# Attention followed by a gated feed-forward: q and k transposed by DMA through DRAM, exact causal widths, and a hand-written order of the two halves

## The chip, the cores and the metric

One core of one Trainium2 chip. The metric is the device time of one execution in microseconds (us), median of the runs. Engines are named as the profile names them: PE (TensorE matmul), PEld (its weight load), DVE (VectorE), ACT (ScalarE), POOL (GpSimd), SP (SyncE, which issues all DMAs here; SPq is its queue). "Clock" is the share of full speed that PE was granted; "DMA share" is the mean busy share of the core's 16 DMA engines, and in short stretches it came out above 1.

## The reference

```python
# q, k, v: (8, 8, 576, 64)   s: (8, 8, 576)   all float32
scores = q @ k^T / sqrt(64)
cum    = cumsum(max(s, 0), axis=-1)
scores = where(j > i, -1e9, scores + min(-(cum[i] - cum[j]), 0))
x      = softmax(scores) @ v            # -> (4608, 512): 8 batches x 576 rows, 8 heads x 64
g      = x @ w_gate                     # (512, 1536)
out    = (g * sigmoid(g) * (x @ w_val)) @ w_out      # (4608, 512)
```

There are 64 heads of 576 rows and nine feed-forward tiles of 512 rows. A batch is eight heads, and a tile needs the whole batch (or batches) its rows lie in. Both halves meet in a DRAM buffer `xdr`: attention writes its rows there, and each tile reads them back transposed as `xt`. In the profiles `sc` are scores, `av` is softmax times v, `pg` and `pv` are the products of `xt` with the gate and value weights, `ht` is what they combine to, and `py` its product with w_out, copied out as the four blocks y0 to y3 (`ysb`). `kt` and `qt` are k and q transposed; `ks` and `qs` are their scratch in DRAM.

## The kernel before

The decay is folded into the scores: q and k are padded from 64 to 68 columns, so that one matmul gives q·k plus the bias. For each head q and k are cast, transposed on PE through PSUM and copied out; the scores are computed over a row length padded to 640. The order of instructions on the engines is left to the framework's scheduler: the program says "one batch of heads, then the tiles that are ready", and the scheduler mixes them.

```python
def do_head(b, h, stg):
    for name, HT, dstT, ptt in (("k", HTK, KT, ptk_tiles), ("q", HTQ, QT, ptq_tiles)):
        nc.any.tensor_copy(pt[:, 0:4, 0:D], main[:, hh, :, :])        # cast to bf16
        nc.any.tensor_copy(pt[:, 4, 0:D], tailt[:, hh, :])
        nc.gpsimd.tensor_copy(pt[:, :, D:DEXT], HT[:, :, bh, :])      # the decay columns
        for c in range(NCH):                                          # NCH = 5
            nc.tensor.transpose(tps[:, c * 128 : (c + 1) * 128], pt[:, c, :], ident)
        nc.any.tensor_copy(dstT, tps)
    ...
    for ch in SCORE_CHUNKS:                                           # rows padded to 640
        ...  nc.tensor.matmul(sc[...], KT[...], QT[...]);  nc.scalar.activation(Pt, sc, AF.Exp)
    for tj in range(NCH):
        nc.vector.tensor_mul(Pt[:, o : o + 128], Pt[:, o : o + 128], keepmask)
    ...  # 15 av matmuls, reciprocal, scaling, two DMAs to xdr per head

def do_moe_tile(tt):
    for c in range(4):
        nc.sync.dma_start_transpose(xt, xdr[tt * TT : (tt + 1) * TT, c * 128 : (c + 1) * 128])
    ...  # 12 x (4 pg + 4 pv matmuls), then 4 x 12 py matmuls, four output DMAs
```

The softmax here doesn't subtract the row's maximum and nothing guards it: scores larger than these inputs give would overflow.

Of the kernel before, what the change touches and what calls it, by code (L numbers as in the profile page):

```python
# [19 lines left out]
def kernel(  # L20
# [11 lines left out]
    nc = tc.nc  # L32

    B, H, S, D = q.shape
    BH = B * H
    NT, DM = out.shape
    DF = moe_w_gate.shape[1]

    SP = 640
    NCH = 5  # L40
    AUG = 4
    DEXT = D + AUG
    HGRP = 4

    PT_OFF = []
    o = 0
    for tj in range(NCH):
        PT_OFF.append(o)
        o += SP - 128 * tj
    PT_TOT = o  # L50

    SCORE_CHUNKS = [
        [(0, 0, 512)],
        [(0, 512, 640), (1, 128, 512)],
        [(1, 512, 640), (2, 256, 640)],
        [(3, 384, 640), (4, 512, 640)],
    ]
# [3 lines left out]
    stage = ctx.enter_context(tc.tile_pool(name="stage", bufs=2))  # L61
    head = ctx.enter_context(tc.tile_pool(name="head", bufs=4))
    small = ctx.enter_context(tc.tile_pool(name="small", bufs=4))
    wpool = ctx.enter_context(tc.tile_pool(name="wpool", bufs=1))
    moes = ctx.enter_context(tc.tile_pool(name="moes", bufs=4))
    hpool = ctx.enter_context(tc.tile_pool(name="hpool", bufs=3))
    xtp = ctx.enter_context(tc.tile_pool(name="xtp", bufs=8))

    apsum = ctx.enter_context(tc.tile_pool(name="apsum", bufs=1, space=bass.MemoryType.PSUM))
    mpsum = ctx.enter_context(tc.tile_pool(name="mpsum", bufs=4, space=bass.MemoryType.PSUM))  # L70

    dram = ctx.enter_context(tc.tile_pool(name="dram", bufs=1, space=bass.MemoryType.DRAM))

    ident = const.tile([128, 128], BF16)
    make_identity(nc, ident)
    keepmask = const.tile([128, 128], BF16)
    make_upper_triangular(nc, keepmask, val=1.0, diag=True)

    NPT = 4
    ptk_tiles = [const.tile([128, NCH, 128], BF16, name=f"ptk{i}") for i in range(NPT)]  # L80
    ptq_tiles = [const.tile([128, NCH, 128], BF16, name=f"ptq{i}") for i in range(NPT)]
    for t in ptk_tiles + ptq_tiles:
        nc.vector.memset(t[:, :, DEXT:128], 0.0)

    spos = prep.tile([BH, SP], FP32)
    nc.vector.memset(spos[:, S:SP], 0.0)
    s_sb = prep.tile([BH, S], FP32)
    nc.sync.dma_start(s_sb, s.flatten_outer_dims())
    nc.scalar.activation(spos[:, 0:S], s_sb, AF.Relu)

    cum_a = prep.tile([BH, SP], FP32)
    cum_b = prep.tile([BH, SP], FP32)
    nc.vector.tensor_copy(cum_a, spos)
    srcs = [cum_a, cum_b]
    cur = 0
    shift = 1
    while shift < S:
        src = srcs[cur]
        dst = srcs[1 - cur]
        nc.vector.tensor_add(dst[:, shift:SP], src[:, shift:SP], src[:, 0 : SP - shift])  # L100
        nc.vector.tensor_copy(dst[:, 0:shift], src[:, 0:shift])
        cur = 1 - cur
        shift *= 2
    cum = srcs[cur]

    c8 = srcs[1 - cur]
    nc.scalar.mul(c8, cum, 8.0)
    hi_bf = prep.tile([BH, SP], BF16)
    nc.vector.tensor_copy(hi_bf, c8)
    lo_f = spos  # L110
    nc.vector.tensor_sub(lo_f, c8, hi_bf)
    lo_bf = prep.tile([BH, SP], BF16)
    nc.vector.tensor_copy(lo_bf, lo_f)
    nhi_bf = prep.tile([BH, SP], BF16)
    nc.scalar.mul(nhi_bf, hi_bf, -1.0)
    nlo_bf = prep.tile([BH, SP], BF16)
    nc.scalar.mul(nlo_bf, lo_f, -1.0)

    HTK = prep.tile([128, NCH, BH, AUG], BF16)
    HTQ = prep.tile([128, NCH, BH, AUG], BF16)  # L120
    nc.vector.memset(HTK[:, :, :, 2:4], 1.0)
    nc.vector.memset(HTQ[:, :, :, 0:2], 1.0)

    def transpose_bh_to_s(src_bf, dst, w):
        for c in range(NCH):
            ps = apsum.tile([128, 64], BF16, tag="tp", bufs=1, name="htp")
            nc.tensor.transpose(ps, src_bf[:, c * 128 : (c + 1) * 128], ident[0:64, 0:64])  # L127
            nc.any.tensor_copy(dst[:, c, :, w], ps)

    transpose_bh_to_s(hi_bf, HTK, 0)  # L130
    transpose_bh_to_s(lo_bf, HTK, 1)
    transpose_bh_to_s(nhi_bf, HTQ, 2)
    transpose_bh_to_s(nlo_bf, HTQ, 3)

    def load_group(b, g):
        h0 = g * HGRP
        stg = {}
        for name, src in (("q", q), ("k", k), ("v", v)):
            main = stage.tile(
                [128, HGRP, 4, D], FP32, tag="stg_" + name, name="stg" + name  # L140
            )
            for c in range(4):
                nc.sync.dma_start(  # L143
                    main[:, :, c, :],
                    src[b, h0 : h0 + HGRP, c * 128 : (c + 1) * 128, :].rearrange(
                        "h p d -> p h d"
                    ),
                )
            tail = stage.tile(
                [128, HGRP, D], FP32, tag="stgt_" + name, name="stgt" + name  # L150
            )
            nc.gpsimd.memset(tail[64:128, :, :], 0.0)
            nc.sync.dma_start(
                tail[0:64, :, :],
                src[b, h0 : h0 + HGRP, 512:576, :].rearrange("h p d -> p h d"),
            )
            stg[name] = (main, tail)
        return stg

    GPB = H // HGRP  # L160
    NGRP = B * GPB
    next_stg = load_group(0, 0)

    WG = [wpool.tile([128, DF], BF16, name=f"wg{c}") for c in range(4)]
    WV = [wpool.tile([128, DF], BF16, name=f"wv{c}") for c in range(4)]
    WO = [wpool.tile([128, DM], BF16, name=f"wo{c}") for c in range(12)]

    def load_weight_piece(i):
        if i < 4:
            c = i  # L170
            wtmp = stage.tile([128, DF], FP32, tag="wld", bufs=2, name="wld")
            nc.sync.dma_start(wtmp, moe_w_gate[c * 128 : (c + 1) * 128, :])
            nc.any.tensor_copy(WG[c], wtmp)
            wtmp2 = stage.tile([128, DF], FP32, tag="wld", bufs=2, name="wld2")
            nc.sync.dma_start(wtmp2, moe_w_val[c * 128 : (c + 1) * 128, :])
            nc.any.tensor_copy(WV[c], wtmp2)
        else:
            for c in range(2 * (i - 4), 2 * (i - 4) + 2):
                wtmp = stage.tile([128, DM], FP32, tag="wld3", bufs=2, name="wld3")
                nc.sync.dma_start(wtmp, moe_w_out[c * 128 : (c + 1) * 128, :])  # L180
                nc.any.tensor_scalar_mul(WO[c], wtmp, 0.5)
    NWPIECE = 10

    xdr = dram.tile([NT, DM], BF16, name="xdr")

    def do_head(b, h, stg):
        bh = b * H + h
        hh = h % HGRP
        KT = head.tile([128, SP], BF16, tag="KT", name="KT")
        QT = head.tile([128, SP], BF16, tag="QT", name="QT")  # L190
        for name, HT, dstT, ptt in (
            ("k", HTK, KT, ptk_tiles),
            ("q", HTQ, QT, ptq_tiles),
        ):
            main, tailt = stg[name]
            pt = ptt[(b * H + h) % NPT]
            nc.any.tensor_copy(pt[:, 0:4, 0:D], main[:, hh, :, :])  # L197
            nc.any.tensor_copy(pt[:, 4, 0:D], tailt[:, hh, :])
            nc.gpsimd.tensor_copy(pt[:, :, D:DEXT], HT[:, :, bh, :])
            tps = apsum.tile([128, SP], BF16, tag="tp", bufs=1, name="tps")  # L200
            for c in range(NCH):
                nc.tensor.transpose(  # L202
                    tps[:, c * 128 : (c + 1) * 128], pt[:, c, :], ident
                )
            nc.any.tensor_copy(dstT, tps)  # L205

        vmain, vtail = stg["v"]
        VT = head.tile([128, NCH, D + 1], BF16, tag="VT", name="VT")
        nc.any.tensor_copy(VT[:, 0:4, 0:D], vmain[:, hh, :, :])
        nc.any.tensor_copy(VT[:, 4, 0:D], vtail[:, hh, :])  # L210
        nc.gpsimd.memset(VT[:, :, D], 1.0)

        Pt = head.tile([128, PT_TOT], BF16, tag="Pt", name="Pt")
        for ch in SCORE_CHUNKS:
            width = sum(e[2] - e[1] for e in ch)
            first_tj = ch[0][0]
            sc = apsum.tile([128, 512], FP32, tag="score", bufs=2, name="sc")
            off = 0
            for (tj, ilo, ihi) in ch:
                w = ihi - ilo  # L220
                nc.tensor.matmul(  # L221
                    sc[:, off : off + w],
                    KT[:, 128 * tj : 128 * (tj + 1)],
# [20 lines left out]
        for bi in range(NCH):  # L244
# [27 lines left out]
            ot[0:64, 4, :],  # L272
        )

    TT = 512
    NTT = NT // TT

    def do_moe_tile(tt):
# [105 lines left out]
```

## Time and profile before

| | us |
|---|---|
| time, median of the first 3 runs | 505.06 (504.21 to 507.08) |
| span of the profiled run | 506.3 |
| PE busy | 442.4 (87%) |
| first feed-forward tile begins | 115.7 |
| one tile with eight heads, once PE is full | 49.5 |
| one tile alone | 31.1 |

The prediction below shows the slices and stretches. From the page, these are the engine totals and the groups that the change touches. The columns of a group are: line, engine, operation, output<-input, count, then busy us, mean ns of one, and the idle time just before with what ended it.

```profile
PE 442.4 (87%) x3364; PEld 237.4 (47%) x3364; DVE 319.3 (63%) x991; ACT 298.2 (59%) x665; POOL 53.2 (11%) x248
...
L292 PE MATMUL pg<-xt,wg 128*128 128x512 bf16 x432 | 123.6, 379 | 2.0 <-DMA xt<-xdr 1.5
...
L239 DVE TENSOR_TENSOR Pt<-Pt,keepmask 128x128 bf16<-128x128 bf16 x320 | 64.5, 221 | 16.5 <-ACT Pt L230 14.5
...
L202 PE MATMUL tps<-ident,ptk 128*128 128x128 bf16 x320 | 31.3, 227 | 13.9 <-ACT ptk L197 13.5
...
L205 DVE COPY KT<-tps 128x640 bf16<-128x640 bf16 x49 | 23.8, 487 | 13.5 <-PE tps L202 13.1
```

The row to keep in mind is the first group: over the whole run PE waited only 1.5 us for `xt`. The transposes (L202, here those of k) and their copies out of PSUM (L205) are the work that the change moves to the DMA engines, and the masks (L239) go from DVE to POOL.

### The profile page before, as it was taken

What the parts mean: (1) busy time and instruction counts of PE and PEld (TensorE: products, weight loads), DVE (VectorE), ACT (ScalarE), POOL (GpSimd) and SP (SyncE); (2) the same over time, 40 slices, a digit from 0 to 9 for tenths busy, and PEclk for the clock granted to TensorE, in tenths of its full rate; (3) what the DMA queues carried; (4) which work ended last, traced back from release to release, by engine and by line L of the source; (5) the groups of instructions that cost most, each with busy time, mean ns of one, the idle gap of its engine ahead of it and who ended that gap; (6) DMA issues with size and microseconds to landing.
All of it is one profiled execution on the core that took longest, in us unless ns stands there. A gap on an engine that the chain in (4) does not pass through costs nothing.

```text
span 506.3 us, 10025 instructions
## 1 busy us (share of the span) xinstructions
PE 442.4 (87%) x3364; PEld 237.4 (47%) x3364; DVE 319.3 (63%) x991; ACT 298.2 (59%) x665; POOL 53.2 (11%) x248
## 2 busy tenths in 40 slices
PE   0277743658999999999999999999999999999997
PEld 0144532433445445554555465546554664444443
DVE  8348853645919846983798278828881887174570
ACT  3568865765439527972796289628952984232331
POOL 2013211110001101210121012102100100000000
PEclk9999985969999999999999999999999999999999
DMA  7805779677756751466255715671641121401102
GB/s 167 245 13 123 197 237 170 175 166 182 171 145 144 150 135 49 99 128 161 69 115 126 179 41 116 135 169 41 131 86 65 34 45 34 124 0 37 48 1 83
DMA packets 181124, 57.44 MB, mean 113 GB/s; under 512 B 173840, under 2 KB 173840, under 8 KB 181072
## 3 DMA queue, kind: packets, MB, share of 16 engines
q1 hardware_dynamic: 181072, 56.80, 46.7%
q8 instruction: 26, 0.43, 0.4%
q14 instruction: 26, 0.21, 0.1%
HBM read 37.90 MB, written 14.16 MB: 103 GB/s over the span
## 4 chain that ended last, share of the span: by engine, by line
PE 70%; DMA 10%; ACT 9%; DVE 4%; SPq 4%; issue 2%; ACTq 0%; POOL 0%; DVEq 0%; POOLq 0%
PE py L320 18%; PE pg L292 17%; PE pv L300 16%; PE sc L221 9%; PE tps L202 5%; PE av L247 5%; ACT Pt L230 4%; DMA wld<-in_moe_w_val_dram 3%; DMA wld<-in_moe_w_out_dram 2%; SPq L143 2%; DMA stgq<-in_q_dram 2%; ACT QT L205 1%; DMA stgtq<-in_q_dram 1%; DMA stgk<-in_k_dram 1%; PE htp L127 1%
## 5 line engine op out<-in xcount | busy, mean ns | idle before, releaser
L230 ACT ACTIVATE Pt<-sc 128x512 bf16<-128x512 f32 (+1 forms) x256 | 133.6, 581 | 14.4 <-PE sc L221 12.7
L292 PE MATMUL pg<-xt,wg 128*128 128x512 bf16 x432 | 123.6, 379 | 2.0 <-DMA xt<-xdr 1.5
L300 PE MATMUL pv<-xt,wv 128*128 128x512 bf16 x432 | 120.9, 379 | 0.0
L308 ACT ACTIVATE th<-pg 128x512 bf16<-128x512 f32 x108 | 65.0, 602 | 74.2 <-PE pg L292 69.2
L221 PE MATMUL sc<-QT,KT 128*128 128x128 bf16 (+3 forms) x448 | 87.5, 285 | 11.1 <-ACT QT L205 3.7
L310 DVE SCALAR_TENSOR_TENSOR pp<-th,pg 128x512 bf16<-128x512 bf16 x108 | 73.7, 683 | 35.9 <-ACT th L308 35.5
L320 PE MATMUL py<-wo,ht 128*128 128x512 bf16 x432 | 94.7, 379 | 0.0
L314 DVE TENSOR_TENSOR ht<-pp,pv 128x512 bf16<-128x512 bf16 x108 | 74.1, 686 | 7.8 <-PE pg L292 0.5
L239 DVE TENSOR_TENSOR Pt<-Pt,keepmask 128x128 bf16<-128x128 bf16 x320 | 64.5, 221 | 16.5 <-ACT Pt L230 14.5
L247 PE MATMUL av<-VT,Pt 128*128 128x65 bf16 x960 | 67.9, 198 | 6.9 <-DVE Pt L239 5.5
L328 ACT COPY ysb<-py 128x512 f32<-128x512 f32 x36 | 21.1, 586 | 79.8 <-PE py L320 75.0
L247 PEld LDWEIGHTS <-Pt 128*128 128x128 bf16 x960 | 48.6, 99 | 38.8 <-DVE Pt L239 30.5
L320 PEld LDWEIGHTS <-ht 128*128 128x128 bf16 x432 | 42.2, 98 | 51.0
L221 PEld LDWEIGHTS <-KT 128*128 128x128 bf16 x448 | 42.0, 98 | 50.3 <-issue 34.4
L300 PEld LDWEIGHTS <-wv 128*128 128x128 bf16 x432 | 40.4, 98 | 37.1 <-issue 2.6
L292 PEld LDWEIGHTS <-wg 128*128 128x128 bf16 x432 | 40.7, 98 | 34.9 <-issue 0.9
L197 DVE CAST ptk<-stgk 128x256 bf16<-128x256 f32 x45 | 12.7, 289 | 53.9 <-PE tps L202 48.6
L202 PE MATMUL tps<-ident,ptk 128*128 128x128 bf16 x320 | 31.3, 227 | 13.9 <-ACT ptk L197 13.5
L202 PE MATMUL tps<-ident,ptq 128*128 128x128 bf16 x320 | 35.3, 226 | 2.6 <-ACT KT L205 1.6
L202 PEld LDWEIGHTS <-ptk 128*128 128x128 bf16 x320 | 24.5, 101 | 20.2 <-ACT ptk L197 13.8
L205 DVE COPY KT<-tps 128x640 bf16<-128x640 bf16 x49 | 23.8, 487 | 13.5 <-PE tps L202 13.1
L259 DVE TENSOR_TENSOR ot<-av,recip 128x320 bf16<-128x320 f32 x64 | 31.1, 486 | 0.7 <-DVE Pt L239 0.3
(65 smaller groups left out, 277.2 us busy)
## 6 DMA issues: line engine op xcount, KB each, us to landing
out_dram<-ysb SPq DMA_DIRECT2D x36, 256.0 KB, 2.1
stgq<-in_q_dram SPq DMA_DIRECT2D x64, 128.0 KB, 3.0
stgk<-in_k_dram SPq DMA_DIRECT2D x64, 128.0 KB, 2.9
stgv<-in_v_dram SPq DMA_DIRECT2D x64, 128.0 KB, 2.8
xdr<-ot SPq DMA_DIRECT2D x64, 64.0 KB, 2.3
wld<-in_moe_w_gate_dram SPq DMA_DIRECT2D x4, 768.0 KB, 5.7
wld<-in_moe_w_val_dram SPq DMA_DIRECT2D x4, 768.0 KB, 6.6
wld<-in_moe_w_out_dram SPq DMA_DIRECT2D x12, 256.0 KB, 3.0
```

Of the source, the lines that this page charges most:

```text
L202: nc.tensor.transpose(tps[:, c * 128 : (c + 1) * 128], pt[:, c, :], ident)
L221: nc.tensor.matmul(sc[:, off : off + w], KT[:, 128 * tj : 128 * (tj + 1)], QT[:, ilo:ihi], start=True, stop=True,)
L230: nc.scalar.activation(Pt[:, pt_lo : pt_lo + width], sc[:, 0:width], AF.Exp, scale=0.125,)
L239: nc.vector.tensor_mul(Pt[:, o : o + 128], Pt[:, o : o + 128], keepmask)
L247: nc.tensor.matmul(av[:, bi * (D + 1) : (bi + 1) * (D + 1)], Pt[:, colo : colo + 128], VT[:, tj, :], start=(tj == 0), stop=(tj == bi),)
L259: nc.vector.tensor_mul(ot, av3[:, :, 0:D], recip[:, :, None].to_broadcast([128, NCH, D]),)
L292: nc.tensor.matmul(pg, WG[c][:, ft * 128 : (ft + 1) * 128], xts[c], start=(c == 0), stop=(c == 3),)
L300: nc.tensor.matmul(pv, WV[c][:, ft * 128 : (ft + 1) * 128], xts[c], start=(c == 0), stop=(c == 3),)
L308: nc.scalar.activation(th, pg, AF.Tanh, scale=0.5)
L310: nc.vector.scalar_tensor_tensor(pp, in0=th, scalar=1.0, in1=pg, op0=ALU.add, op1=ALU.mult)
L314: nc.vector.tensor_mul(ht, pp, pv)
L320: nc.tensor.matmul(py, hts[ft][:, ts_ * 128 : (ts_ + 1) * 128], WO[ft], start=(ft == 0), stop=(ft == 11),)
```

## The change

Its intent is to take work off PE, DVE and ACT. (1) q and k of four heads are cast on POOL, written to DRAM scratch and read back by a transposing DMA, in place of PE transposes. (2) Scores are computed over 576 rows and not 640, and the four full diagonal blocks are masked by one POOL select. (3) The scheduler is switched off: the order on every engine, SP's queue included, is that of the program text, with attention running `LAG` = 1.5 heads ahead of feed-forward. The diff also has something that the intent does not name: the rows of a batch go to `xdr` in one pair of DMAs after its last head, and no longer in a pair for each head, and `xt` is one transposing DMA and not four.

```diff
-    SP = 640
+    # exact widths: 1600 columns of scores a head, diagonal blocks together
+    CHUNKS = [
+        [(0, 0, 128), (1, 128, 256), (2, 256, 384), (3, 384, 512)],
+        [(0, 128, 576), (3, 512, 576)],
+        [(1, 256, 576), (2, 384, 576)],
+        [(4, 512, 576)],
     ]
 ...
+    with tc.manual_schedule():
+        def scratch(hb):                        # hb: a group of four heads
+            for C, SC in ((CK, KS), (CQ, QS)):
+                nc.sync.dma_start(SC[hb].rearrange(...), C[hb % 2].rearrange(...))
+        def transposes(hb):
+            nc.sync.dma_start_transpose(KT[hb % 2][:, 0 : HB * S], KS[hb])
+            nc.sync.dma_start_transpose(QT[hb % 2], QS[hb])
 ...
-        for c in range(NCH):
-            nc.vector.tensor_mul(... keepmask)
+            if ci == 0:
+                nc.gpsimd.affine_select(pt[:, 1088:1600], ...)
 ...
+        def side(hb, step):                     # step: which of the four heads
+            if hb + 1 < NHB:
+                if step == 0:
+                    if hb + 2 < NHB:
+                        load_qk(hb + 2)
+                        if hb % 2 == 0:
+                            load_v((hb + 2) // 2)
+                    aug(hb + 1, nc.gpsimd); ...     # casts of k
+                if step == 1:
+                    ...                             # casts of q
+                    scratch(hb + 1)
+                if step == 2:
+                    transposes(hb + 1)
 ...
+        def ffn_items(tt):
+            xt = xtp.tile([128, 4, TT], BF16, tag="xt", name="xt")
+            nc.sync.dma_start_transpose(xt, xdr[tt * TT : (tt + 1) * TT, :])
+            ...                                 # pg, pv, py matmuls, one yield each
+        LAG = 1.5
+        for tt in range(NTT):
+            ...
+            for _ in ffn_items(tt):
+                pump(lo + (hi - lo) * min(1.0, n / span))    # heads in between
```

The five v loads of a batch, the outputs y0 to y3 of a tile, `xdr`, the scratch and `xt` all stand in one queue, SP's, in the order in which this text comes to them. `xt` of a tile is issued when its first item is asked for, and that is after the last output of the tile before.

## The prediction

> **What bounds the kernel now.** I read the page first (busy shares and the forty slices), then a table of three stretches, then the order of time inside a mixed stretch, then the issue queue.
>
> ```profile
> span 506.3 us, 10025 instructions
> PE   0277743658999999999999999999999999999997
> PEclk9999985969999999999999999999999999999999
> ```
>
> The page: TensorE (PE) is full from about slice 10, and ragged before it, with a lowered clock in places. So there are two regimes.
>
> ```profile
> 0.00:126.00 126.00, 68.51 (x656) 42.90 (x657) 72.88 (x270) 81.66 (x185) 21.11 (x97) 0.89 0.68 167
> 126.00:440.40 314.40, 311.71 (x2423) 166.47 (x2422) 213.43 (x674) 196.95 (x448) 32.08 (x151) 1.00 0.47 108
> 440.40:502.60 62.20, 62.20 (x289) 27.99 (x286) 33.02 (x48) 19.02 (x32) 0.00 (x0) 1.00 0.09 35
> ```
>
> Stretches (us, then PE, weight load, DVE, ACT, POOL busy, clock, DMA share, GB/s). Before 126 us PE is half idle and DMA is the busiest (0.68). After it PE sets the end: 311.7 of 314.4 us. The last 62.2 us are two feed-forward tiles alone, 31.1 us each.
>
> ```profile
> 250.05 0.33 PE L202 MATMUL tps<-ident,ptq 128*128 128x128 bf16 x3
> 250.21 0.59 PE L292 MATMUL pg<-xt,wg 128*128 128x512 bf16 x2
> 251.29 0.35 PE L247 MATMUL av<-VT,Pt 128*128 128x65 bf16 x6
> 251.91 0.44 PE L202 MATMUL tps<-ident,ptk 128*128 128x128 bf16 x5
> ```
>
> A busy time is latency and overlaps its neighbours, so I take the spacing. Two 512-column matmuls take 0.59 us and one 0.379, so one costs 0.216 us (0.42 ns a column). Six av take 0.35 us at 0.198 each: 0.030 apart. Five transposes take 0.44 at 0.219: 0.055 apart.
>
> ```profile
> 429.47 5.20 SPq L282 DMA_TRANSPOSE xt<-xdr  x4
> ...
> 429.92 4.26 PE L320 MATMUL py<-wo,ht 128*128 128x512 bf16 x19
> ```
>
> The input of the next tile (xt) is fetched while the py matmuls of this tile still run: it is prefetched. That matters below.
>
> DMA rates, each GB/s over DMA share:
>
> ```profile
> 4.00:20.00 16.00, 1.41 (x7) 0.73 (x8) 12.22 (x37) 7.09 (x21) 1.26 (x6) 1.00 0.88 200
> 65.00:71.00 6.00, 3.95 (x52) 2.42 (x49) 3.75 (x13) 4.46 (x9) 0.86 (x2) 1.00 0.77 237
> 405.00:406.00 1.00, 1.00 (x13) 0.65 (x10) 0.98 (x5) 1.00 (x4) 0.00 (x0) 1.00 0.58 131
> 436.00:439.00 3.00, 3.00 (x16) 1.35 (x15) 0.00 (x0) 0.59 (x1) 0.00 (x0) 1.00 0.41 155
> ```
>
> 256 B loads 227 GB/s, weight loads 308, transposes 226, output writes 378.
>
> [...] The trace agrees for the engines (226 against 227 GB/s with 256 B rows), not for the issue: 1.2 us for 512 rows against 0.5 us for a plain DMA. [...]
>
> ```profile
> 72.00:82.00 10.00, 1.03 (x15) 0.87 (x15) 2.98 (x13) 4.12 (x7) 0.31 (x1) 0.53 1.00 212
> 82.00:89.70 7.70, 5.40 (x43) 3.91 (x44) 3.67 (x19) 5.10 (x12) 1.80 (x10) 0.50 0.71 139
> ```
>
> PE stood 8.3 us there, and the clock stayed at half to 89.7.
>
> **The change part by part.** (1) PE per head. Before: scores 1920 columns x 0.42 ns = 0.81 us, ten transposes 0.55, fifteen av 0.45: 1.81 us. After: 1600 columns 0.68, no transposes, av 0.45: 1.13. A tile (144 matmuls, 31.1 us) with eight heads falls from 45.6 (the trace shows 49.5 per period) to 40.1 us. Over seven such periods that is 66 us of possible gain.
>
> (2) DVE and ACT lose the casts, the KT/QT copies (about 0.5 and 0.7 us, 128 of them) and, to POOL, the masking (320 x 0.22 us). They have slack in the mixed part anyway (DVE 213 and ACT 197 of 314 us), so this only helps. POOL gets one 128x512 and one 128x64 select per head and the casts. A 128x128 select took 0.29 us; my estimate from that is 0.7 us for the large one, 20 to 25 us in a period. It is not the bound.
>
> (3) DMA gains 18.9 MB of scratch writes and 18.9 MB of transposed reads on 56.8 MB. For four heads: k and q loads 1.18 MB at 300 GB/s (taking the weight rate for long rows), 3.9 us; scratch write 3.1; transposes 5.2. For a batch, v 5.2; xdr 1.6; xt 2.3; output 2.8. A batch: 2 x 12.2 + 11.9 = 36 us against 40 us of PE. It fits, if it is spread.
>
> (4) The start. First scores need s, k, q, casts, scratch, and also wait for v0, k1 and q1, which SP issues ahead of the first transposes. The first DMA is issued at 0.7 us and a plain one takes about 1.4 us to begin (2.1 us landing of an output less 0.7 of data); s and k, q (0.5 + 3.9) have landed by 7.5, casts 1.7, so the scratch is issued at 9.2. Then 9.2 + 1.4 + 3.1 + 5.2 + 3.9 + 5.2 + 0.6 = 28.6 us, like now. Then, in SP's order up to the first xt: k2 q2 3.9, v1 5.2, scratch 3.1, four weight pairs 4 x 5.1, transposes 5.2, k3 q3 3.9, scratch 3.1, transposes 5.2, k4 q4 3.9, v2 5.2, xdr 1.6, scratch 3.1, xt 2.3: 66 us. With 5 us for waits between scratch and transposes, feed-forward begins at about 99 us, with 9.5 heads behind it; now it runs densely from 126.
>
> (5) The tile boundary. The order of the built program has, on SP, around each boundary: y0, k, q, v (five DMAs), y1, y2, xdr, two scratch writes, y3, xt. So xt is issued only when y3, the last output of the tile before, has been computed, and PE's next instruction after that tile's last py is pg, which needs xt. PE is in order: attention cannot fill the hole. Floor of the hole: copy of y 0.6, issue 0.4, xt with four times the data of the present one (2.7 us landing, 0.9 of it data, now 2.3) 4.1, and 0.3 for semaphores: 5.5 us. With the load burst: y0 is done 30.5 us into a period, so (copy 0.6, issue 0.4, 1.4 to begin) the queue starts at 33 with y0 0.7, k q 3.9, v 5.2, y1 y2 1.4, xdr 1.6: 46; scratch 3.1 and y3 0.7: 50; xt 2.3 and landing: near 52 against 40.1 of PE, a hole of 12. Some of the y and scratch may be out earlier; I take 10.5 us. [...] Five boundaries have the burst; the sixth has scratch alone (7); the last two have neither (5.5).
>
> Sum: start 99; late wo casts in DVE's order 3; five periods 5 x 52.1 = 260.5; 40.1 + 7 + 1.5 = 48.6; the seventh with 7.5 us of attention 38.6 + 7 = 45.6; 31.1 + 7 = 38.1; last tile and its output 34. Total 528.8; I say 528.
>
> **Rivals.** (a) PE bound throughout, holes negligible: 99 + 7 x 40.1 + 62.2 + 3 = 445 us. For it speaks the saturated PE of now; against it that now xt is prefetched, and here it cannot be. (b) Only the floor of each hole, loads drained early: 99 + 342 + 8 x 5.5 + 3 = 488[...]. For it: DMA totals fit in the period. Against: SP reaches the loads only behind y0. (c) Transposes of 2304 rows take SP longer to issue than my 3.4 us (of the present 1.15 us for 512 rows I take 0.5, a plain issue, as fixed and 0.65 as growing with rows; fully proportional it would be 5.2): k and q then come after the heads that need them, DMA and SP become the bound, about 555 us. (d) POOL three times slower than estimated would hold the av matmuls: above 560.
>
> **Range and chances.** The floors (PE 342, eight holes 44, output 3, a start of at least 80) give 470, so a large gain is nearly excluded. The middle case is 528; (b) is the good end, (c) the bad one. Range 495 to 556. Faster by 2% (under 495): 0.14; within 2%: 0.22; slower: 0.64.
>
> **What would show it.** After: PE busy near 342 us plus about 20 at the start by spacing, and the chain of waits naming xt at eight places. In order of time, between the last py of a tile and the next pg: idle of 5 to 12 us, ended by the xt DMA, longest where v was loaded. SP: y3 just before xt. Clock slices under 9 after 100 us. If pg never waits for xt, step 5 is wrong and 445 to 480 is near; if sc waits for kt or qt inside tiles, (c) holds; if av waits for POOL's pt, (d).

Statements about the chip that no trace or run of this case shows are cut from this text, and the cuts are marked. With them go terms of the forecast. The sum came to 528.8 with 1.5 us for the lowered clock at each of the eight boundaries (within each of the five 52.1, as the 1.5 of the sixth, within the 7 of the last two): 12 us, not worked out from the trace; in the stretch quoted the clock stayed at half for 7.7 us after PE restarted at 82.0. Without them the sum is 516.8, still just over 2% slower. What was measured after stands under "The cold clock" below.

"The trace agrees for the engines" compares two numbers of the trace, 226 GB/s for transposes and 227 for plain loads of 256-byte rows. That a DMA waits behind all that SP issued before it was not isolated by any run; where (4) and (5) add up transfers in SP's order, that is the author's estimate. Other things that the prediction counts on are shown by later runs. PE is in order: at a boundary of the kernel after, the nine `av` matmuls that come behind the first `pg` had their last input, POOL's select, at 193.37 us, and PE stood from 193.4 to 206.19 and ran them only behind that `pg`, at 207.85. The "0.3 for semaphores": the chain of such a floor in the run with more lead alone has 0.32 us between its pieces (0.21, 0.02, 0.05 and 0.04).

## The result and the profile after

| | before | after |
|---|---|---|
| time, median of 4 runs each, us | 505.79 | 548.55 (546.96 to 549.58) |
| ratio, fast runs | 1 | 1.0835 (95%: 1.0798 to 1.0872) |
| span of the profiled run, us | 506.3 | 545.3 |
| PE busy, us | 442.4 | 384.4 |
| mean granted clock of PE in the profiled run | 0.973 | 0.861 |
| DMA bytes, MB | 57.44 | 95.00 |

A ratio here is made from the fast runs of both kernels, so it is not quite the ratio of the medians quoted. The kernel became 8.4% slower with 58 us less of PE busy time.

From the page of the kernel after: totals, slices (each digit a fortieth of the span), the chain that ended last by line, and the costliest group.

```profile
PE 384.4 (71%) x2834; PEld 205.5 (38%) x2834; DVE 206.5 (38%) x373; ACT 199.8 (37%) x404; POOL 127.0 (23%) x272
...
PE   0031342899389918992999189928993998697797
...
PEclk9995565799889968996899689968996999799799
DMA  6999989967973897379647974897349102202202
...
PE pg L353 19%; PE pv L366 18%; PE py L377 17%; DMA xt<-xdr 10%; PE sc L242 7%; DMA xdr<-ot 5%; PE av L277 5%; DMA qt<-qs 2%; DMA wld<-in_moe_w_val_dram 2%; POOL pt L255 1%; SPq L193 1%; DMA s_sb<-in_s_dram 1%; ACT ysb L385 1%; SPq L115 1%; POOL ck L176 1%
...
L353 PE MATMUL pg<-xt,wg 128*128 128x512 bf16 x432 | 121.0, 406 | 92.4 <-DMA xt<-xdr 92.4
```

Where PE was a row of nines, it now has a notch at each boundary between two tiles, with one in the clock beside it. The chain that sets the end holds 15% of `xt` and `xdr` transfers. The group of the first matmul of a tile (L353) says why: 92.4 us of idle time, all ended by `xt`. In the kernel before the same group had 1.5 us.

What PE waited for in the kernel after, from the view of waits (total us, times, longest):

```profile
PE pg L353 <- DMA xt<-xdr: 92.4, 9, 13.9
PE av L277 <- DVE ot L294: 27.7, 4, 14.2
PE sc L242 <- DMA qt<-qs: 26.2, 2, 21.7
```

Nine waits for nine tiles. The other two rows lie before 82 us, in the start. The nine, in order of time, are 12.28 (the start's), 10.28, 12.80, 10.21, 13.93, 12.37, 8.49, 5.90 and 6.13 us.

Stretches of the kernel after (us, then PE, weight load, DVE, ACT, POOL busy, clock, DMA share, GB/s):

```profile
0.00:100.00 100.00, 24.00 (x231) 18.01 (x232) 21.99 (x42) 20.55 (x45) 29.36 (x62) 0.71 0.99 261
100.00:250.00 150.00, 125.05 (x1000) 67.92 (x998) 66.70 (x123) 70.24 (x144) 46.56 (x99) 0.91 0.80 207
```

The first 100 us belong to the DMA engines (share 0.99). After that nothing is full: PE 125 of 150 us, DMA 0.80. Two resources with room and a time that is still too long is the mark of an order problem.

Here is one boundary as the chain of waits has it, in order of time (start us, us, what):

```profile
193.07 0.22 issue
193.28 0.59 ACT ysb L385
...
194.25 4.67 DMA xdr<-ot
...
198.93 7.22 DMA xt<-xdr
...
206.19 1.86 PE pg L353 x4
```

and what SP issued around it:

```profile
185.26 5.62 SPq L115 DMA_DIRECT2D rawv<-in_v_dram  x4
190.98 2.01 SPq L120 DMA_DIRECT2D rawvt<-in_v_dram  x1
...
194.25 0.41 SPq L301 DMA_DIRECT2D xdr<-ot  x1
...
197.50 1.18 SPq L386 DMA_DIRECT2D out_dram<-ysb  x1
198.93 4.03 SPq L347 DMA_TRANSPOSE xt<-xdr  x1
```

SP was occupied with the five v loads from 185.26 to 192.99. The last head's `ot`, which `xdr` takes, was computed by 190.7 (the order of time has its scaling at 190.19, 0.49 us long), but its DMA went out only at 194.25, 3.5 us later, while the DMA engines were full (share 1.18 from 191.0 to 194.2); it took 4.67 us to land, and `xt`, which has to wait for it and stands behind y3 as well, took another 7.22. PE stood from 193.4, just after its last py, to 206.19: its next instruction was the `pg` that needs `xt`, and the nine `av` behind it, whose last input (POOL's select, from 193.13, 0.24 us long) was there at 193.37, ran only after that `pg`, at 207.85. (Of the hole, 4.67 and 7.22 us are the landings of `xdr` and `xt`. In the kernel before, by the medians of its page, the 64 KB that one head sends to `xdr` landed in 2.3 us, and here the 512 KB of a batch in 4.6. No run sent the rows to `xdr` head by head in this order, so what that would have saved is open.)

The clock in and after the same hole, in two stretches of the kernel after (columns as above):

```profile
195.70:206.10 10.40, 0.00 (x0) 0.00 (x0) 0.00 (x0) 0.00 (x0) 0.00 (x0) 0.50 1.04 270
206.20:209.40 3.20, 3.20 (x16) 1.49 (x16) 0.68 (x2) 0.60 (x1) 0.00 (x0) 0.50 1.17 221
```

PE restarted at half clock and had the full one only 3.2 us later (1.00 in the stretch that follows), so it did 1.6 us less work than it could have (the first four `pg` took 1.86 us, four at full clock from 209.94 took 1.03). After the eight holes the clock record stays at half for 3.2 to 5.7 us, 32.7 us together, which by the same reckoning is 16 us of work or 2.0 us a hole. In the 10.4 us before, no compute engine did anything; only the DMA engines worked.

### The profile page after: what moved, and what is told of

It reads as the page before. It is cut to its first block, busy times and chain, and to the rows that moved or that the text cites. A ratio compares the mean times of both kernels' runs of the same rounds, so it can differ in the third digit from the quotient of the medians.

```text
span 545.3 us, 7406 instructions
## 1 busy us (share of the span) xinstructions
PE 384.4 (71%) x2834; PEld 205.5 (38%) x2834; DVE 206.5 (38%) x373; ACT 199.8 (37%) x404; POOL 127.0 (23%) x272
## 4 chain that ended last, share of the span: by engine, by line
PE 67%; DMA 19%; POOL 3%; SPq 3%; issue 3%; ACT 2%; DVE 1%; ACTq 0%; POOLq 0%; DVEq 0%
PE pg L353 19%; PE pv L366 18%; PE py L377 17%; DMA xt<-xdr 10%; PE sc L242 7%; DMA xdr<-ot 5%; PE av L277 5%; DMA qt<-qs 2%; DMA wld<-in_moe_w_val_dram 2%; POOL pt L255 1%; SPq L193 1%; DMA s_sb<-in_s_dram 1%; ACT ysb L385 1%; SPq L115 1%; POOL ck L176 1%
## 5 line engine op out<-in xcount | busy, mean ns | idle before, releaser
L353 PE MATMUL pg<-xt,wg 128*128 128x512 bf16 x432 | 121.0, 406 | 92.4 <-DMA xt<-xdr 92.4
L251 ACT ACTIVATE pt<-sc 128x512 bf16<-128x512 f32 (+1 forms) x256 | 117.5, 505 | 115.1 <-PE sc L242 115.0
L255 POOL TENSOR_SCALAR_AFFINE_SELECT pt<-pt 128x512 bf16<-128x512 bf16 x64 | 41.4, 647 | 288.5 <-ACT pt L251 288.5
L242 PE MATMUL sc<-qt,kt 128*128 128x128 bf16 (+4 forms) x576 | 79.0, 256 | 26.8 <-DMA qt<-qs 26.2
L353 PEld LDWEIGHTS <-wg 128*128 128x128 bf16 x432 | 39.6, 102 | 130.5 <-issue 89.2
L277 PE MATMUL av<-vt,pt 128*128 128x65 bf16 x960 | 57.8, 204 | 30.9 <-DVE ot L294 27.7
L277 PEld LDWEIGHTS <-pt 128*128 128x128 bf16 x960 | 51.2, 104 | 63.4 <-issue 35.7
L242 PEld LDWEIGHTS <-kt 128*128 128x128 bf16 x576 | 49.4, 106 | 63.4 <-DMA kt<-ks 19.6
L366 PEld LDWEIGHTS <-wv 128*128 128x128 bf16 x432 | 39.3, 102 | 36.3 <-issue 6.9
L293 DVE RECIPROCAL rc<-av 128x5 f32<-128x5 f32 x64 | 12.2, 190 | 59.0 <-PE av L277 59.0
L294 DVE TENSOR_TENSOR ot<-av,rc 128x320 bf16<-128x320 f32 x64 | 31.5, 492 | 2.2
L260 POOL TENSOR_SCALAR_AFFINE_SELECT pt<-pt 128x64 bf16<-128x64 bf16 x64 | 16.7, 261 | 32.7 <-ACT pt L251 31.9
L176 POOL CAST ck<-rawk 128x576 bf16<-128x576 f32 x32 | 20.5, 669 | 0.1
L176 POOL CAST cq<-rawq 128x576 bf16<-128x576 f32 x30 | 19.1, 666 | 0.0
L199 POOL CAST vt<-rawv 128x512 bf16<-128x512 f32 x28 | 17.1, 642 | 0.0
```

The source lines that it names most:

```text
L176: eng.tensor_copy(dst[:, r, :, 0:D], loaded[name, hb][:, r, :, :])
L242: nc.tensor.matmul(sc[:, o : o + w], kt[:, hh * S + 128 * tj : hh * S + 128 * (tj + 1)], qt[:, hh * S + lo : hh * S + hi], start=True, sto ...
L251: nc.scalar.activation(pt[:, CHUNK_PT[ci] : CHUNK_PT[ci] + o], sc[:, 0:o], AF.Exp, scale=0.125)
L255: nc.gpsimd.affine_select(pt[:, 1088:1600], pt[:, 1088:1600], pattern=[[0, 4], [1, 128]], compare_op=ALU.is_ge, fill=zreg, base=0, channel ...
L277: nc.tensor.matmul(av[:, bi * (D + 1) : (bi + 1) * (D + 1)], pt[:, c0 : c0 + 128], VT[b % 2][:, tj, h, :], start=(tj == 0), stop=(tj == bi),)
L294: nc.vector.tensor_mul(ot[:, :, h * D : (h + 1) * D], av3[:, :, 0:D], rc[:, :, None].to_broadcast([128, NCH, D]),)
```

## The experiments

The theory: the loss is at the boundary, because `xt` is late in SP's queue, behind the v burst and the outputs. The rivals: the DRAM traffic of q and k is itself too much; the halved clock is the main part; attention is simply too little ahead.

### Two moves in SP's queue, each alone and together

Loads later: the loads of the group that starts a batch go behind the transposes and `xt`.

```diff
-                    if hb + 2 < NHB:
+                    if hb + 2 < NHB and (hb % 2 == 1 or hb == 0):
                         load_qk(hb + 2)
 ...
                     transposes(hb + 1)
+                    if hb + 2 < NHB and hb % 2 == 0 and hb >= 2:
+                        load_qk(hb + 2)
+                        load_v((hb + 2) // 2)
```

> Edit: from the third group of four heads on, the k, q and v loads of an even group are issued after the transposes of that group (behind xt) instead of ahead of y1, y2 and xdr. Theory 1 (the hole is the wait of xt in SP's order): xdr is issued right after its data, some 7 us earlier; holes at xt1 to xt5 fall from 10.2 to 13.9 us to about 6 to 8, the first xt comes 5 us earlier, total 548 - 5*5 - 5 = 515 to 525 us. Theory 2 (total DMA work sets the period): the same bytes, so the time stays at 545 to 550 and kt or qt is waited for instead.

Measured: 538.67 us, ratio 1.0636 (1.0588 to 1.0684). Less than expected. What PE waited for:

```profile
PE pg L356 <- DMA xt<-xdr: 70.8, 9, 9.2
...
PE pv L369 <- DVE ht L374: 8.9, 1, 8.9
```

The holes shrank by 21.6 us altogether, to 7.8 to 9.2 us where the v burst had been, but 8.9 us came back as a new wait in the first tile: the second load of w_out now stood behind v (issued at 110.45 us, in the kernel after at 104.19), and its cast stands in DVE's order before the `ht` that PE needs.

`xt` sooner: it is issued directly behind `xdr`, not when the tile asks for it.

```diff
                 nc.sync.dma_start(xdr[b * S + 512 : (b + 1) * S, :], ot[0:TAIL, 4, :])
+                load_xt(b)
+                if b == B - 1:
+                    load_xt(b + 1)
 ...
-            nc.sync.dma_start_transpose(xt, xdr[tt * TT : (tt + 1) * TT, :])
+            xt = xts.pop(tt)
```

> Edit: xt is issued directly behind xdr, ahead of the two scratch writes and y3; loads stay where they were. Theory 1: xt still waits for xdr, which waits behind v, so only the 2 to 3 us that xt spends behind scratch and y3 go (xt takes 5.8 to 7.5 us now, 4.7 undisturbed); the last two holes shrink too as their xt is no longer behind y3: total 548 - 6*2.5 - 2*5 = 520 to 530 us. Theory 2: unchanged, 545 to 550.

Measured: 521.84 us with the slow run, 519.92 without it; 1.0291 (1.0225 to 1.0357), about as expected.

```profile
PE pg L362 <- DMA xt<-xdr: 65.7, 8, 11.8
```

After the start, holes of 8.7 to 10.0 us remained before five tiles, then 5.2 and 1.7 us, and none before the last.

Both edits together, and nothing else:

```diff
+                load_xt(b)                       # behind xdr
+                    if hb + 2 < NHB and hb % 2 == 0 and hb >= 2:    # behind the transposes
+                        load_qk(hb + 2)
+                        load_v((hb + 2) // 2)
```

> Both edits. Theory 1: xdr leaves at about 38.5 us of a period, lands 2.5 us later, xt 4.5 us after that: holes of about 5 us, 490 to 505 us in total. If the two gains were not independent (a third wait behind them), more than 510. Theory 2: 545 to 550.

Measured: 504.82 us, 0.9988 (0.9954 to 1.0022): all that was lost against the kernel before is back, with not one instruction taken away. PE's longest wait in sum:

```profile
PE pg L365 <- DMA xt<-xdr: 42.2, 8, 8.5
```

The holes after the start are 5.2 to 5.9 us, 1.8 before the last tile but one, and none before the last. The wait for w_out in the first tile is here too (11.0 us). The holes are what is left because the batch's last head is finished so late in the tile: `xdr` has to land and `xt` has to land after it.

### Attention further ahead, alone

> After with attention 3.5 heads ahead instead of 1.5, nothing else. My theory: xt is still issued only behind y3, so a floor of 5 to 7 us stays in all eight holes (about 45 us together, from 92), however far attention is ahead; and the transposes of a group come in after's place, so sc waits for qt by 1 to 4 us in most groups as in the run with lag and both moves: 510 to 535 us. The rival, that attention being too little ahead is the cause of the holes, says: no wait of pg for xt, 450 to 490 us.

```diff
-        LAG = 1.5
+        LAG = 3.5
```

Measured: 527.7 us, 1.045 (1.0406 to 1.0495), as my theory expected, though of its two parts one failed: `sc` waited for `qt` only in the start (24.5 us in 3 waits).

```profile
PE pg L353 <- DMA xt<-xdr: 65.5, 9, 16.2
```

The holes stayed, at 5.7 to 7.4 us in the eight boundaries (the 16.2 us lie before the first tile). One of them in the chain of waits of this run:

```profile
300.58 0.59 ACT ysb L385
...
301.57 4.73 DMA xt<-xdr
...
306.34 1.86 PE pg L353 x4
```

Here `xdr` does not appear in the chain: it had landed before. What remains is the copy of y3, its issue and then `xt`: 5.67 us, where the prediction had put the floor of a hole at 5.5. No lead of attention removes it, as long as `xt` is issued behind y3. So the rival "attention is too little ahead" does not explain the holes alone, though the lead takes 27 us off the total of 92.

### Both moves and attention further ahead

The two edits above and this:

```diff
-        LAG = 1.5
+        LAG = 3.5
```

> Both edits, and attention runs 3.5 instead of 1.5 heads ahead of the tile that needs it, so xt has about 10 us more. Theory 1: no holes, so no half clock after them either: 98 + 280 + 59 + 3 = 440 to 455 us, faster than both kernels. If DMA or kt/qt is the next bound (theory 2 as the second limit): 465 to 490, with sc waiting for kt or qt.

Measured: 519.47 us, 1.0258 (the two moves alone had 504.82). The expected 440 to 455 us failed by 65 us; the expectation's second case named the wait that came (`sc` for `qt`), but not its size (465 to 490 us). PE's waits:

```profile
PE sc L242 <- DMA qt<-qs: 61.5, 14, 22.0
...
PE pg L365 <- DMA xt<-xdr: 7.2, 2, 5.2
```

The holes at `xt` were gone, as foreseen, and a new wait stood in their place: in eleven of the thirteen groups of heads from the fourth on, `sc` waits 1.6 to 4.9 us for `qt`. In SP's order of time the scratch of one such group was issued at 224.15, the transpose that has to wait for it at 231.78, and the score followed at 240.02: 16 us for a chain that starts three heads before its use. The waits came in groups whose loads had been moved and in groups whose loads had not, so the later loads alone are not their cause. In the run with the lead alone, which kept its holes, they did not come; this fits the reading that the time had been hidden there, while PE stood at `xt`.

### The whole chain earlier

So the chain load, cast, scratch, transpose was moved: casts and scratch one group of heads earlier, transposes at the start of the group before their use, loads at its third head, the w_out casts later in DVE's order; `xt` behind `xdr` and LAG 3.5 as above.

```diff
         def side(hb, step):
+            if step == 0:
+                if hb + 1 < NHB:
+                    transposes(hb + 1)
+                if hb + 2 < NHB:
+                    aug(hb + 2, nc.gpsimd)
+                    cast_one(hb + 2, "k", 0, nc.gpsimd); ...
+            if step == 1 and hb + 2 < NHB:
+                ...
+                scratch(hb + 2)
+            if step == 2:
+                if hb + 3 < NHB:
+                    load_qk(hb + 3)
+                if hb % 2 == 0 and hb + 2 < NHB:
+                    load_v((hb + 2) // 2)
```

> e4 lost its gain to qt: 14 waits of scores for qt, 61 us in all, because the chain casts, scratch, transposes (16 us in the loaded queue) starts three heads before it is needed. Edit on e4: casts and scratch of a group run one group earlier, its transposes at the start of the group before; and the casts of w_out stand later in DVE's order (e4 lost 13.6 us there, pv waiting for ht). Theory 1 (latency of the chain): qt waits after 100 us vanish (under 5 us), the total is 440 to 470 us. Rival (DMA volume, share 0.81 in the mixed part of e4, sets the period): about 500, with the waits moved to xt, raw loads or POOL.

Measured: 456.34 us (454.41 to 459.06), 0.9022 (0.8993 to 0.9051), correct. It beats the kernel after by 92 us and the kernel before by 49. PE's slices on its page:

```profile
PE   0031423659869999999999999999999989999996
```

and what PE still waited for, and a stretch of its mixed part (columns as before):

```profile
PE sc L247 <- DMA qt<-qs: 21.6, 1, 21.6
PE pg L368 <- DMA xt<-xdr: 6.1, 2, 5.1
...
150.00:380.00 230.00, 225.89 (x1849) 125.04 (x1885) 124.51 (x234) 130.19 (x266) 76.79 (x167) 1.00 0.87 217
```

From 150 us PE is full at full clock while the same 95.00 MB move at a DMA share of 0.87. A tile with eight heads takes 40.24 us (four in a row); the prediction had 40.1 for PE alone. So the rival "the traffic is too much" is refuted for the mixed part: the change's arithmetic was sound, its order was not. Against the run before, two things changed at once, the chain and the w_out casts: the wait for `qt` fell from 61.5 to 21.6 us (all of it in the start), and the one for `ht`, 13.6 us there, is gone, with 3.3 us for a w_out cast in its place. The two were not run apart.

### The halved clock alone

Unread matmuls in the eight holes keep PE busy; nothing else changes.

```diff
+            if tt > 0:
+                pd = mp.tile([128, TT], FP32, tag="m", name="pd")
+                for _ in range(42 if tt < 6 else 32 if tt == 6 else 20):
+                    nc.tensor.matmul(pd, WG[0][:, 0, 0:128], WO[0][:, 0, :], start=True, stop=True)
```

> Changed kernel with matmuls that nobody reads (42, 32 or 20 of 512 columns, 9, 7, 4.3 us) in each of the eight holes, nothing else. The holes stay, the clock should not fall. If the half clock after a hole costs what the records say (3.2 to 5.6 us at half speed, so 1.6 to 2.8 us each): 548 - 8*2 = 530 to 536 us, granted clock well over 0.861. If the lowered clock is only a record and costs nothing, 546 to 550.

Measured: 536.3 us, at the upper edge of what was expected, 1.0593 (1.0551 to 1.0634), granted clock 0.935 in place of 0.861. Against 1.0835 that is 0.0242 of 505.8, or 12.2 us, 1.5 us a hole.

What PE still waited for:

```profile
PE pg L359 <- DMA xt<-xdr: 29.8, 9, 12.7
```

Of these 29.8 us 12.7 lie before the first tile, which has no unread matmuls; before the others PE was idle for 1.2 to 2.9 us. The clock is a real part of the loss but not its main part. (In the eight holes of the kernel after, by its clock record, the clock fell 2.2 to 4.9 us after PE had stopped, and it rose 3.2 to 5.7 us after the restart.)

### The widths alone

The kernel before, with scores over 576 rows and the masks cut to what is used; the last block of Pt is padded with 64 zeros.

```diff
-        o += SP - 128 * tj
+        o += S - 128 * tj
 ...
-        [(3, 384, 640), (4, 512, 640)],
+        [(3, 384, 576), (4, 512, 576)],
 ...
+            w = min(128, S - 128 * tj)
             nc.vector.tensor_mul(
-                Pt[:, o : o + 128], Pt[:, o : o + 128], keepmask
+                Pt[:, o : o + w], Pt[:, o : o + w], keepmask[:, 0:w]
             )
```

> The kernel before with one part of the change alone: exact causal widths, 1600 instead of 1920 score columns per head. PE saves 320 x 0.42 = 0.135 us per head; about 48 heads lie in the PE-bound part: 6 us, and ACT some more in the start: 497 to 501 us (ratio 0.98 to 0.99). If the holes of the schedule swallow it: 504 to 507.

Measured, in five rounds: 502.19 us, 0.9932 (0.9915 to 0.9949). That is 3.4 to 3.7 us, less than expected. A mixed tile fell from 49.5 to 48.3 us, which is eight heads of 0.14 us; the start gave part of it back (the first tile began at 117.5 and not 115.7 us).

### PE transposes in the kernel after

Is the way through DRAM worth having? First attempt: the kernel after with q and k transposed on PE and copied out by DVE.

```diff
+                nc.tensor.transpose(ps[:, j - j0, :], C[:, r, j, :], ident)
+            dst = T[:, r * 1152 : (r + 1) * 1152].rearrange("c (q j) -> c j q", j=J)
+            nc.vector.tensor_copy(dst[:, j0:j1, :], ps[:, 0 : j1 - j0, :])
```

> Changed kernel with the DRAM part undone: q and k transposed on PE as before (36 transposes of 0.055 us per four heads, copied out by DVE), no scratch. Order of the rest unchanged. Theory 1: the start loses two scratch and transposed trips (about 8.3 us each of the queue's time, three groups before the first xt), so feed-forward begins near 75 to 80 us instead of 98; the holes lose only the scratch in front of xt (3 us in six of them); PE gains 4 us a period: 548 - 20 - 18 + 26 = 530 to 542. If the DRAM trips were the main cost of the change: under 510.

Measured: 756.88 us, 1.4953. This says nothing on the question, because of a defect of my edit. The group of the larger copies of q (those of k are like it; as many of 128x512 take 2.4 us each):

```profile
L198 DVE COPY qt<-tps 128x640 bf16<-128x640 bf16 x32 | 94.8, 2963 | 12.0 <-PE tps L196 10.4 <-PE sc L253 1.6
```

A copy that took 0.487 us in the kernel before takes 2.96 us here, where the layout with nine rows to a partition makes its output step over nine elements. 344 us of DVE copies became the bound. (The next run has the same copies without the step, at 0.487 us, so it is the step that costs; why it costs this much is not shown.)

Second attempt: a contiguous copy, so that the rows of a head come in another order, and the decay set to zero so that nothing overflows. Its output is wrong, which doesn't matter for the time.

```diff
-            dst = T[:, r * 1152 : (r + 1) * 1152].rearrange("c (q j) -> c j q", j=J)
-            nc.vector.tensor_copy(dst[:, j0:j1, :], ps[:, 0 : j1 - j0, :])
+            o = r * 1152 + 128 * j0
+            nc.vector.tensor_copy(T[:, o : o + 128 * (j1 - j0)], ps[:, 0 : j1 - j0, :].rearrange("c j q -> c (j q)"))
 ...
-        nc.scalar.activation(sp8, s_sb, AF.Relu, scale=8.0)
+        nc.scalar.activation(sp8, s_sb, AF.Relu, scale=0.0)
```

> After's order, but q and k are transposed on PE and copied out of PSUM without a stride (the defect of the run before it), so the scratch writes and the transposed reads of them are gone. The result is wrong on purpose: the rows of a head come in another order and the decay is set to zero, so that nothing overflows; the work per instruction is the same. PE pays 9 transposes of 0.055 us per head, about 4 us per tile of eight heads, DVE about 1 us of copies per head. My theory (xt is issued behind y3 and the v burst) says: the start shrinks by about 15 us because the queue carries 12 us less there, the five large holes shrink by the scratch that stood in the queue and by the wait for it, to 7 to 9 us, PE gets 28 us more: 525 to 560 us, so no verdict against the DRAM path in this order. The rival (the scratch traffic itself makes the holes) says: all holes at 5.5 us, total about 520.

Measured: 557.7 us, 1.1017 (1.099 to 1.1044), no faster than the kernel after. PE's waits:

```profile
PE pg L370 <- DMA xt<-xdr: 72.0, 9, 9.6
PE tps L196 <- DVE kt L198: 32.4, 34, 9.4
```

With the scratch and its transposes gone (57.32 MB in place of 95.00), holes of 8.4 to 9.6 us remain in front of the first six tiles. In front of the same tiles the kernel after has 10.2 to 13.9 us. So the traffic of q and k adds some 1 to 5 us to a hole, and most of the hole is there without it. The start was 15.8 us shorter (first tile at 82.1 us), as expected. The second row is a cost of my edit (one PSUM buffer for the transposes; it also leaves one score buffer fewer), so the 557.7 is somewhat too high; without all of these 32.4 us it would still be about 525, and not near 456.

### PE transposes in the best kernel

The same edit in the kernel of 456.34 us: no scratch, and the transposes spread over the group before. Its output is wrong, which doesn't matter for the time.

```diff
-                nc.sync.dma_start(SC[hb].rearrange(...), C[hb % 2].rearrange(...))
-            nc.sync.dma_start_transpose(KT[hb % 2][:, 0 : HB * S], KS[hb]); ...
+                        if bh // HB + 1 < NHB:
+                            for i in TR_AT.get((bh % HB, ci), ()):
+                                tr_half(bh // HB + 1, i)     # on PE, copied out by DVE
```

> The best kernel so far (456.3 us) with q and k transposed on PE and copied out of PSUM without a stride, wrong on purpose as above. It is PE-bound from about 140 us, so 0.5 us of transposes per head cost 4 us per tile, about 25 us over the mixed part; the start may win 5 to 15 us since its DMA engines carry less. Mine: 462 to 482 us, that is, once the queue is in order the DRAM path is worth 1 to 6 per cent. The rival, that the DRAM path costs more than it saves even there, says: under 450 us. One score buffer fewer in PSUM (two instead of three) is part of this edit and could cost a little.

Measured: 455.32 us, 0.8996 (0.8978 to 0.9014), against 0.9022 (0.8993 to 0.9051): the same within the intervals. I had expected 462 to 482. The first stretch of this run:

```profile
0.00:100.00 100.00, 66.78 (x663) 47.85 (x664) 60.55 (x120) 40.59 (x83) 47.80 (x99) 0.88 0.79 226
```

Two effects cancel. The first tile begins at 70.9 us and not at 95.7, since the DMA engines have less to move in the start (0.79 and not 1.01). Each tile with eight heads takes 46.02 us and not 40.24. My sum had 5 to 15 us for the first and 4 us a tile for the second; both were too small. So the way through DRAM wins 5.8 us in each mixed tile against this version and costs 25 us once, in the start. Not all of either is DRAM traffic. From 71 us on, PE waits 6.6 us altogether for the copy out of the one PSUM buffer, about 1 us a tile, which a version with two buffers might save. And of the 25 us, 8.6 lie before the first scores (20.67 and not 29.25 us), where the DMA share of the best kernel is 0.92 and the way through scratch is a chain of waits.

### The start of the best kernel

The casts of the gate and value weights one piece (1.4 heads) later in DVE's order.

```diff
-            if i < NWCH:
-                wq.pop(0)()
+            if 1 <= i < NWCH + 1:
+                only_cast(i - 1)
+            if i < NWCH:
+                only_load(i)
```

> The best kernel so far (456.3 us) with the DVE casts of each pair of gate and value weights one piece (1.4 heads) later in DVE's order. If the start is bound by the DMA engines (share 0.99 there), feed-forward begins at 94 to 97 us as before and the time is 450 to 459 us. If it is bound by DVE standing in order before the weight casts (av waited 33 us for ot there), feed-forward begins 8 to 20 us sooner and the time is 435 to 448 us.

Measured: 459.9 us, 0.9088 (0.9065 to 0.911). First tile at 98.9 us, 3.2 us later than in the best kernel, and the time is just over the 450 to 459 expected. The start's stretch in this run:

```profile
0.00:100.00 100.00, 25.71 (x269) 19.34 (x270) 22.99 (x46) 23.65 (x52) 32.46 (x72) 0.75 1.01 260
```

With a DMA share of 1.01, DVE's order was not what held the start: the new order won nothing and cost some 3 us. This and the run before agree: from the first scores on, the start is bound by the DMA engines (in the best kernel their share is 1.05 from 29 to 95.7 us). That points to a version not run: the first groups of heads transposed on PE, the later ones by DMA. My estimate from the two runs is up to 25 us less than 456, if both effects add; it is open.

## Why the prediction was right

The direction and the mechanism held: slower, with a hole in front of each tile because `xt` stands behind y3 and the v burst. The time was 20 us over the predicted 528, inside the range. Term by term, with the first matmul of each tile as the mark:

| term of the sum | predicted, us | measured, us |
|---|---|---|
| start, to the first tile | 99 | 97.9 |
| w_out casts in DVE's order | 3 | no such wait in this kernel |
| five periods | 5 x 52.1 = 260.5 | 53.4, 54.9, 52.2, 57.1, 54.3 = 271.8 |
| sixth | 48.6 | 50.6 |
| seventh | 45.6 | 47.9 |
| eighth | 38.1 | 39.3 |
| last tile and its output | 34 | 37.8 |
| sum | 528.8 | 545.3 (the profiled span) |

- **Step 1, PE a head.** Right: without holes a tile with eight heads takes 40.24 us (the best kernel), predicted 40.1. Its share for the widths holds too: the run with the widths alone gave 0.14 us a head at PE, and the step has 0.13 (0.81 less 0.68). The whole kernel got only 3.4 to 3.7 us of the 8 or so that 64 heads would make, since its start grew.
- **Step 2, the other engines.** Right. The large select took 0.647 us (predicted 0.7), and POOL held PE once, for 3.2 us in the start.
- **Step 3, DMA fits if it is spread.** Right, and shown: the same bytes with PE full at a DMA share of 0.87.
- **Step 4, the start.** 97.9 for 99, with some luck: the sum has a slip of 1 us (0.7 + 1.4 + 0.5 + 3.9 make 6.5, not 7.5), and 5 us for waits were put in without a working. The finer part, that it is the DMA engines which bound it, is shown by the share of 0.99 and by the two runs that changed the start.
- **Step 5, the hole.** The mechanism is shown by four runs: taking v away from in front shrinks it, `xt` sooner shrinks it, both leave the floor, and more lead alone leaves 5.7 to 7.4 us. SP did stand in the wait for `xdr`: it issued `xt` at 198.93, when `xdr` had landed (194.25 + 4.67). The size was short. The full count had given 12 us, although its "xt 2.3 and landing" adds only the 2.3 to 49.6; with the 1.8 us of landing that the floor has (2.7 less 0.9) it would be nearly 14. It was then discounted to 10.5, in the hope that some of the y and scratch would be out earlier. The five holes were 10.28, 12.80, 10.21, 13.93 and 12.37, mean 11.9: the discount was wrong, 7 us over the five. The count also left out SP's own time. It sized v by its data (5.2 us), and SP stood 7.7 us issuing it, so that `xdr` went out 3.5 us after it could have. In the boundary shown, `xdr` landed 47.6 us and `xt` 54.8 us into the period; the count has 46 and 52.
- **The cold clock.** The sum had 1.5 us a restart, an assumption (see the note at the prediction). The mean period less its hole is 42.5 us, 2.2 over the 40.24 of a period without holes; the run with unread matmuls gave 1.5 back; by the clock record half speed cost 2.0 a hole, the clock being low for 4.1 us on average (32.7 us after eight holes). So the term was short by up to half a microsecond.
- **The last tile.** The 34 us have 31.1 and about 3 for the output; they leave out that this tile too starts at half clock (for 5.6 us by the clock record). Its last py ended at 541.56, 34.0 us after its first matmul, which is 2.9 us over the 31.1, and the output took the other 3.7 (as in the kernel before, 502.6 to 506.3).

Of the rivals, (a) and (b) did not come, but they are what the order could have had: 456 us is the best kernel, between 445 and 488. (c) did not come: kt took 2.2 to 7.2 us to issue and qt 2.2 to 3.6, with medians of 3.2 and 2.5 (the prediction took 3.4), and in the kernel after `sc` waited for `qt` only twice, before 82 us. It came in another kernel, once the holes were gone, by 1.6 to 4.9 us a group. (d) did not come.

## What to carry to other kernels

With a hand-written order, the issue queue has to be ordered with the same care as an engine (here two moves in it took 548.55 us to 504.82): look for the transfer that the next stage needs first, and ask what stands in front of it, both as bytes and as issue time (the v loads held SP for 7.7 us, for data of 5.2). A hole hides the waits behind it, so mend the chain as a whole (here `xt` behind its source, more lead, and the preparation one group earlier) and measure again after each step. Work moved from a full engine to the DMA engines was paid where these were full already, here in the first 100 us (DMA share 0.99; in the best kernel the first tile began at 95.7 us, and at 70.9 with the transposes on PE).
